# Transposing pooled k and scaled v by DMA on the sync queue instead of on TensorE

## The chip, the cores and the metric

One core of one Trainium2 chip. The metric is the device time of one execution in microseconds; lower is better. Each comparison uses runs interleaved with runs of the kernel before on the same chip.

## The reference, cut to what matters

```python
def _attn_ref(q, k, v, phi):                 # 8 batches, 8 heads, 576 rows, 64 columns, 32 memory slots
    a = softmax(phi)                         # over the 32 slots
    k_m = np.einsum('bhsm,bhsd->bhmd', a, k) # pooled k: 32 rows a head
    v_m = np.einsum('bhsm,bhsd->bhmd', a, v)
    attn = softmax(scale * np.matmul(q, k_m.transpose(0, 1, 3, 2)))
    return np.matmul(attn, v_m)

def _moe_ref(x, g_ln, w_ch1, w_ch2):         # x: the heads side by side, 512 columns
    xn = (x - mu) / np.sqrt(var + 1e-06) * g_ln
    return x + np.maximum(xn @ w_ch1, 0.0) @ w_ch2
```

The scores need k_m with its columns on the partitions, and the first layer, which the kernel merges with v_m, needs v_m the same way, scaled by the gain g_ln. So each batch needs three 128x128 transposes: two for k, one for v.

## The kernel before

The kernel works on one batch after the other and weaves the attention of batch nb into the second layer's matmuls of batch b = nb - 1. Every engine runs its instructions in the order in which they are written here, and so does the sync queue with its DMAs.

```python
def a_tr(b, ...):                      # the transposes on TensorE
    t_ps = big([P, 3, P], BF16, "kvT_ps")
    for g in range(2):
        nc.tensor.transpose(t_ps[:, g, :], s["k2"][:, g]..., ident)
    nc.tensor.transpose(t_ps[:, 2, :], s["v2"]..., ident)
    nc.vector.tensor_copy(out=kvT[:, 0:2, :], in_=t_ps[:, 0:2, :])
    nc.vector.tensor_tensor(out=kvT[:, 2, :]..., in0=t_ps[:, 2, :]..., in1=g_bf..., op=ALU.mult)
    ...
# one turn of the main loop (cut)
half(0)                                # eight matmuls of the second layer
a_kv(nb)                               # pooled k and v into PSUM, copied out
x_tiles(pr, t[0:2], False); x_tiles(pr, t[2:4], False)
phis[nb + 1] = load_phi(nb + 1)        # sync queue
load(nb + 1)                           # GpSimd queue: k, v, q of the batch after next
half(1)
a_tr(nb)
x_stats(...)
a_qT(nb + 1, 0)                        # q's transpose, a DMA on the sync queue already
half(2)
a_sc(nb)                               # scores: the first reader of kvT
...
mm2_out(pr, t[0])                      # result tile, stored from the sync queue
...
a_vb(nb)                               # products on GpSimd
```

The softmax here doesn't subtract the row's maximum and nothing guards it: scores larger than these inputs give would overflow.

Of the kernel before, what the change touches and what calls it, by code (L numbers as in the profile page):

```python
# [9 lines left out]
FP32 = mybir.dt.float32  # L10
BF16 = mybir.dt.bfloat16
AF = mybir.ActivationFunctionType
ALU = mybir.AluOpType
# [3 lines left out]
def kernel(  # L17
# [11 lines left out]
    nc = tc.nc  # L29

    B, H, S, D = q.shape
    M = phi.shape[3]
    C = H * D
    F = moe_w_ch1.shape[1]
    P = 128
# [14 lines left out]
    consts = ctx.enter_context(tc.tile_pool(name="consts", bufs=1))  # L50
    inp = ctx.enter_context(tc.tile_pool(name="inp", bufs=2))
    att = ctx.enter_context(tc.tile_pool(name="att", bufs=2))
# [3 lines left out]
    def big(shape, dtype, name):  # L56
        return psum.tile(shape, dtype, name=name, tag="big", bufs=3)

    def one(shape, dtype, name):
        return psum.tile(shape, dtype, name=name, tag="one", bufs=2)  # L60
# [8 lines left out]
    def load_phi(b, queue=None):  # L69
        t = inp.tile([P, 4, NS * M], FP32, name="phi_st")  # L70
        (queue or nc.sync).dma_start(out=t, in_=phi[b].rearrange("(j e) (p c) m -> (e p) j (c m)", e=2, p=TS))
        return t
# [23 lines left out]
    def load(b):  # L96
        loaded[b] = (phis[b] if b > 2 else load_phi(b, nc.gpsimd), load_kv(b), load_q(b))
# [16 lines left out]
    ident = consts.tile([P, P], BF16, name="ident")  # L114
# [28 lines left out]
    loaded[1] = (phi1, kv1, q1)  # L143

    g_bf = consts.tile([P, 4], BF16, name="g_bf")
    gneg = consts.tile([P, 4, P], BF16, name="gneg")
    m_sb = consts.tile([P, F], FP32, name="m_sb")

    def gain():
        g4b = consts.tile([4, P], BF16, name="g4b")  # L150
        nc.vector.tensor_copy(out=g4b, in_=g4)
        g_ps = one([P, 4], BF16, "g_ps")
        nc.tensor.transpose(g_ps, g4b, ident[0:4, 0:4])
        nc.vector.tensor_copy(out=g_bf, in_=g_ps)
        nc.vector.tensor_scalar(out=gneg, in0=g_bf.unsqueeze(2).to_broadcast([P, 4, P]),
                                scalar1=-1.0 / C, scalar2=None, op0=ALU.mult)

# [19 lines left out]
    st8 = {}  # L177
# [21 lines left out]
    def kv_mm(b, ps, sl, js=range(4)):  # L199
        e, kv = st8[b]["e"], st8[b]["kv"]  # L200
        for c in range(NS):
            for j in js:
                for g in range(2):
                    r = TS * g
                    nc.tensor.matmul(  # L205
                        ps[32 * j:32 * (j + 1), g, 0:D * (sl.stop - sl.start)],
                        e[r:r + TS, c, j, :], kv[r:r + TS, j, sl, D * c:D * (c + 1)],
                        start=(c == 0), stop=(c == NS - 1), tile_position=(r, 32 * j))

    def kv_sum(b, ps):  # L210
        e = st8[b]["e"]
        for c in range(NS):
            nc.tensor.matmul(ps[:, 0, P:P + 2], e[:, c].rearrange("p j m -> p (j m)"), ones8,
                             start=(c == 0), stop=(c == NS - 1))

    def k_out(b, k_ps, on_act):
        k2 = att.tile([P, 2, 2, D], BF16, name="k2")
        k_in = k_ps[:, :, 0:D].unsqueeze(2).to_broadcast([P, 2, 2, D])
        if on_act:
            nc.scalar.activation(out=k2, in_=k_in, func=AF.Copy)  # L220
        else:
            nc.vector.tensor_copy(out=k2, in_=k_in)  # L222
        st8[b]["k2"] = k2

    def v_out(b, v_ps):
        v2 = att.tile([P, 2, D], BF16, name="v2")
        nc.vector.tensor_copy(out=v2, in_=v_ps)
        st8[b]["v2"] = v2

    def rs_out(b, ps):  # L230
        rs = att.tile([P, 2], FP32, name="rs", bufs=4)
        nc.vector.reciprocal(out=rs, in_=ps[:, 0, P:P + 2])  # L232
        st8[b]["rs"] = rs

    def a_kv(b):
        ps = big([P, 2, 512], FP32, "kv_ps")
        if b < 2:
            kv_sum(b, ps)
        else:

            for i in range(2):
                nc.tensor.matmul(ps[:, 0, P:P + 2], st8[b]["es"][:, i, :], ones8,
                                 start=(i == 0), stop=(i == 1))
        kv_mm(b, ps, slice(0, 2))
        k_out(b, ps, b < 2)
        v_out(b, ps[:, :, D:2 * D])
        rs_out(b, ps)

    def a_tr(b, k_part=True, v_part=True):
        s = st8[b]  # L250
        t_ps = big([P, 3, P], BF16, "kvT_ps")
        if k_part:
            kvT = att.tile([P, 3, P], BF16, name="kvT")
            s["kvT"] = kvT
            for g in range(2):
                nc.tensor.transpose(t_ps[:, g, :], s["k2"][:, g].rearrange("p a d -> p (a d)"), ident)
        kvT = s["kvT"]
        if v_part:
            nc.tensor.transpose(t_ps[:, 2, :], s["v2"].rearrange("p a d -> p (a d)"), ident)  # L259
        if k_part:  # L260
            nc.vector.tensor_copy(out=kvT[:, 0:2, :], in_=t_ps[:, 0:2, :])  # L261
        if v_part:
            nc.vector.tensor_tensor(out=kvT[:, 2, :].rearrange("p (j m) -> p j m", m=M),
                                    in0=t_ps[:, 2, :].rearrange("p (j m) -> p j m", m=M),
                                    in1=g_bf.unsqueeze(2).to_broadcast([P, 4, M]), op=ALU.mult)
            rsum = att.tile([P, 2], FP32, name="rsum")
            nc.vector.tensor_reduce(out=rsum, in_=s["v2"], axis=mybir.AxisListType.X, op=ALU.add)
            s["rsum"] = rsum
# [166 lines left out]
    def mm2(pr, t, j0, j1, ps=None, finish=True):  # L435
        rT = pair[pr]
        if j0 == 0:
            chs[(pr, t)] = one([P, C], FP32, "ch_ps") if ps is None else ps
        ch_ps = chs[(pr, t)]
        for j in range(j0, j1):  # L440
            nc.tensor.matmul(ch_ps, rT[:, j, P * t:P * (t + 1)], w2b[:, j, :],  # L441
                             start=(j == 0), stop=(j == JC - 1))
        if j1 == JC and finish:
            mm2_out(pr, t)
# [113 lines left out]
    for b in range(1, B):  # L558
        pr, nb = b // 2, b + 1
        odd = b % 2  # L560
        t = [4, 5, 6, 7, 8] if odd else [0, 1, 2, 3]
        more = nb < B
        last = not more


        mm1(b, 0, 4)
        for f in late[0:1]:
            f()
        mm1(b, 4, 7)
        for f in late[1:2]:  # L570
            f()
        mm1(b, 7, JC)
        for f in late[2:]:
            f()
        late = []

        def half(i):
            if not (last and i >= 8):
                mm2(pr, t[i // 2], 8 * (i % 2), 8 * (i % 2 + 1), finish=False)

        half(0)
        if more:
            a_kv(nb)
        x_tiles(pr, t[0:2], False)
        x_tiles(pr, t[2:4], False)
        if nb + 1 < B:
            phis[nb + 1] = load_phi(nb + 1)
            load(nb + 1)
        half(1)
        if more:  # L590
            a_tr(nb)
        x_stats(pr, t[0])
        x_stats(pr, t[1])
        if nb + 1 < B:
            a_qT(nb + 1, 0)
        half(2)
        if more:
            a_sc(nb)
        x_rstd(pr, t[0:2])
        if more:  # L600
            a_w1b(nb, 0)
        mm2_out(pr, t[0])
        half(3)
        if more:
            a_den(nb, finish=False)
        mm2_out(pr, t[1])
        x_stats(pr, t[2])
        if odd or last:
            x_stats(pr, t[3])
            x_rstd(pr, t[2:4])  # L610
        half(4)
        if more:
            a_den2(nb)
        if odd:
            x_tiles(pr, t[4:5], False)
        else:
            a_w1b(nb, 1)
            a_w1b(nb, 2)
            a_w1b(nb, 3)
        if more:  # L620
            a_vb(nb)
        half(5)
        if odd or last:
            mm2_out(pr, t[2])
        if nb + 1 < B:
            a_exp(nb + 1)
        half(6)
        if odd:
            if more:
                a_w1b(nb, 1)  # L630
                a_w1b(nb, 2)
                a_w1b(nb, 3)
            x_stats(pr, t[4])
            x_rstd(pr, t[4:5])
        half(7)
        if odd:
            mm2_out(pr, t[3])
            half(8)
            half(9)
            if last:  # L640
                mm2_last(pr, t[4])
            else:
                late = [lambda pr=pr, tt=t[4]: mm2_out(pr, tt)]
        else:
            x_stats(pr, t[3])

            def tail(pr=pr, tt=t[2:4]):
                x_rstd(pr, tt)
                mm2_out(pr, tt[0])
            late = [tail, lambda pr=pr, tt=t[3]: mm2_out(pr, tt)]  # L650
# [30 lines left out]
```

## Time and profile before

| | before |
|---|---|
| time, median of 3 runs | 253.57 us (253.17 to 253.96) |
| span of the profiled run | 251.5 us |
| busy: TensorE, VectorE, ScalarE, GpSimd | 94%, 62%, 50%, 24% |
| granted TensorE clock | 1.00 |
| transposes of k and v | 24 on TensorE, 219 ns a record |
| transposes of q by DMA | 6 of 20 tiles each, 4.9 us to landing |

Landing is the time from a DMA's issue until its reader sees that it is complete. The granted clock is the share of its full clock that TensorE is given.

TensorE is busy nearly all the time, but a pipelined matmul's record is longer than the time it adds: those of the second layer last 379 ns on average and follow each other by 214 ns in the chain. What an instruction is worth is read from the chain of waits in order of time, which the prediction shows together with the DMA share around it.

### The profile page before, as it was taken

To read this page: it belongs to the slowest core of one execution; us is meant where nothing else is said; L and a number is where in the kernel's file an instruction comes from. 1 tells how busy PE (TensorE), PEld (TensorE's weight loads), DVE (VectorE), ACT (ScalarE), POOL (GpSimd) and SP (SyncE) were. 2 spreads that over 40 slices of the span, in tenths; PEclk is the share of its full clock that TensorE was granted. 3 is DMA by queue.
4 is the path that set the end of the run, shared out by engine and by line. 5 is a ranking of instruction groups with operands and counts; after the bars stand their busy time and mean duration, and the time that the engine had idled before them with its cause. 6 is when DMAs were issued, how large, how long until landed. Compare 5 with 4: busy or idle time off the path is not lost.

```text
span 251.5 us, 5775 instructions
## 1 busy us (share of the span) xinstructions
PE 236.7 (94%) x2422; PEld 133.1 (53%) x2453; DVE 154.9 (62%) x300; ACT 125.3 (50%) x213; POOL 60.0 (24%) x99
## 2 busy tenths in 40 slices
PE   7868999799999999999999999999999999999993
PEld 2533555347544665467544674467444764476453
DVE  3236772595397655967479636965679537963641
ACT  3155662587354464737363646555561755265220
POOL 8632230027204502170206302360205011000000
PEclk9999999999999999999999999999999999999999
DMA  7999999998997898639963997359871300303133
GB/s 151 194 206 206 206 256 218 281 207 122 219 191 145 155 253 189 142 43 197 241 135 80 142 252 174 85 75 231 202 145 42 80 8 0 86 16 69 44 84 83
DMA packets 41922, 36.82 MB, mean 146 GB/s; under 512 B 17444, under 2 KB 37160, under 8 KB 41896
## 3 DMA queue, kind: packets, MB, share of 16 engines
q0 software_dynamic: 17248, 19.53, 45.7%
q1 hardware_dynamic: 24488, 16.79, 28.4%
q8 instruction: 19, 0.31, 0.5%
q10 hardware_dynamic: 160, 0.13, 0.2%
q14 instruction: 7, 0.06, 0.1%
HBM read 41.42 MB, written 9.44 MB: 202 GB/s over the span
## 4 chain that ended last, share of the span: by engine, by line
PE 72%; DMA 17%; ACT 5%; DVE 2%; issue 2%; POOL 1%; POOLq 0%
PE ch_ps L441 41%; PE h_ps L372 22%; DMA q_bf<-in_q_dram 7%; DMA w2b<-in_moe_w_ch_dram 6%; ACT E_sb L313 4%; DMA kv_bf<-in_k_dram 3%; PE w1b_ps L351 2%; PE o_ps L402 2%; DVE x_sb L465 2%; PE kv_ps L205 2%; PE last_ps L453 1%; PE sc_ps L308 1%; POOL q_bf L92 1%; ACT rstd L428 1%; ACT rstd L427 0%
## 5 line engine op out<-in xcount | busy, mean ns | idle before, releaser
L441 PE MATMUL ch_ps<-w2b,rT 128*128 128x512 bf16 x531 | 123.4, 379 | 3.2 <-issue 1.7
L441 PEld LDWEIGHTS <-rT 128*128 128x128 bf16 x560 | 52.1, 98 | 63.8 <-issue 7.0
L378 ACT ACTIVATE rT<-h_ps 128x576 bf16<-128x576 f32 x88 | 52.5, 648 | 30.6 <-PE h_ps L372 30.4
L372 PE MATMUL h_ps<-Eh,w1b 128*128 128x288 bf16 x512 | 66.7, 285 | 0.7 <-ACT rT L378 0.5
L372 PEld LDWEIGHTS <-w1b 128*128 128x128 bf16 x512 | 49.6, 97 | 17.3 <-issue 1.9
L380 DVE TENSOR_SCALAR rT<-h_ps 128x576 bf16<-128x576 f32 x40 | 30.3, 758 | 30.1 <-PE h_ps L372 29.4
L355 DVE SCALAR_TENSOR_TENSOR w1b<-m_sb,rsum,w1b_ps 128x512 bf16<-128x512 f32 x64 | 43.8, 743 | 6.8 <-PE w1b_ps L351 3.8
L465 DVE SCALAR_TENSOR_TENSOR x_sb<-ch_ps,rstd,x_sb 128x512 f32<-128x512 f32 x35 | 25.6, 744 | 8.6 <-PE ch_ps L441 6.9
L408 ACT ACTIVATE x_sb<-o_ps 128x1024 f32<-128x1024 f32 (+1 forms) x20 | 17.8, 933 | 18.4 <-PE o_ps L402 18.4
L421 DVE BATCH_NORM_STATS2 bst<-x_sb 128x6 f32<-128x512 f32 x36 | 24.3, 676 | 3.1 <-ACT x_sb L408 3.1
L189 POOL TENSOR_TENSOR es<-e_sb 128x512 f32<-128x512 bf16 x6 | 6.9, 1154 | 66.2 <-ACT e_sb L182 66.2
L276 POOL TENSOR_TENSOR vb<-v,vmask 128x256 bf16<-128x256 bf16 x12 | 7.7, 662 | 59.4 <-DVE rs L232 59.4
L313 ACT ACTIVATE E_sb<-sc_ps,rs 128x640 bf16<-128x640 f32 x16 | 11.8, 790 | 19.6 <-PE sc_ps L308 19.6
L427 ACT ACTIVATE rstd<-mv,eps_sb 128x2 f32<-128x2 f32 (+1 forms) x20 | 5.9, 296 | 30.0 <-DVE mv L422 30.0
L337 DVE SCALAR_TENSOR_TENSOR Eh<-E_sb,rs,rden 128x576 bf16<-128x576 bf16 x16 | 12.4, 815 | 4.9 <-ACT rden L336 4.8
L327 ACT ACTIVATE rden<-den_ps 128x576 f32<-128x576 f32 x16 | 9.6, 648 | 3.6 <-PE den_ps L325 3.6
L174 PE MATMUL w_ps<-fill 128*128 128x512 f32 x14 | 9.2, 778 | 1.6 <-DVE fill L119 1.6
L351 PE MATMUL w1b_ps<-w1r,kvT 64*32 64x512 bf16 x256 | 10.7, 381 | 0.0
L222 DVE CAST k<-kv_ps 128x256 bf16<-128x256 f32 x7 | 3.0, 424 | 12.5 <-PE kv_ps L205 12.5
L182 ACT ACTIVATE e_sb<-phi_st 128x1152 bf16<-128x1152 f32 x8 | 9.3, 1156 | 2.6 <-DMA phi_st<-in_phi_dram 2.6
L261 DVE COPY kvT<-kvT_ps 128x256 bf16<-128x256 bf16 x8 | 2.3, 292 | 12.5 <-PE kvT_ps L259 11.8
L336 ACT ACTIVATE rden<-rden 128x576 f32<-128x576 f32 x16 | 10.0, 676 | 0.0
(69 smaller groups left out, 151.2 us busy)
## 6 DMA issues: line engine op xcount, KB each, us to landing
out_dram<-x_sb SPq DMA_DIRECT2D x70, 128.0 KB, 2.5
kv_bf<-in_k_dram POOLq DMA_DIRECT2D x7, 576.0 KB, 6.8
kv_bf<-in_v_dram POOLq DMA_DIRECT2D x7, 576.0 KB, 9.7
phi_st<-in_phi_dram SPq DMA_DIRECT2D x6, 576.0 KB, 8.9
q_bf<-in_q_dram POOLq DMA_DIRECT2D x6, 576.0 KB, 13.2
w1r<-in_moe_w_ch_dram POOLq DMA_DIRECT2D x4, 512.0 KB, 14.1
w2b<-in_moe_w_ch_dram POOLq DMA_DIRECT2D x4, 512.0 KB, 19.0
q_bf<-in_q_dram POOLq DMA_DIRECT2D x4, 288.0 KB, 12.5
```

The costliest lines, as they stand in the source:

```text
L313: nc.scalar.activation(out=E_[:, g].rearrange("p (a x) -> p a x", a=2), in_=sc[:, :, 0:HP], func=AF.Exp, scale=s["rs"][:, g:g + 1])
L336: nc.scalar.activation(out=rd[:, g], in_=rd[:, g], func=AF.Exp, scale=-1.0)
L337: nc.vector.scalar_tensor_tensor(out=Eh[:, g, :], in0=s["E"][:, g, 0:S], scalar=s["rs"][:, g:g + 1], in1=rd[:, g].rearrange("p a x -> p (a ...
L351: nc.tensor.matmul(ps[32 * j:32 * (j + 1), g, :], s["kvT"][r:r + 64, 2, 32 * j:32 * (j + 1)], w1r[r:r + 64, j, fs], start=True, stop=True, ...
L355: nc.vector.scalar_tensor_tensor(out=s["w1b"][:, g, fs], in0=m_sb[:, fs], scalar=s["rsum"][:, g:g + 1], in1=ps[:, g, :], op0=ALU.mult, op1 ...
L372: nc.tensor.matmul(h_ps[:, half, 0:HS], s["w1b"][:, g, P * j:P * (j + 1)], s["Eh"][:, g, HS * half:HS * (half + 1)], start=(g == 0), stop= ...
L378: nc.scalar.activation(out=dst, in_=h_ps[:, :, 0:HS], func=AF.Relu)
L380: nc.vector.tensor_scalar(out=dst, in0=h_ps[:, :, 0:HS], scalar1=0.0, scalar2=None, op0=ALU.max)
L408: nc.scalar.activation(out=x[:, 0:n].rearrange("p i (u y) -> p i u y", u=2), in_=o_ps.rearrange("p u (i y) -> p i u y", i=2)[:, 0:n], func ...
L421: nc.vector.bn_stats(out=stt, in_=x)
L441: nc.tensor.matmul(ch_ps, rT[:, j, P * t:P * (t + 1)], w2b[:, j, :], start=(j == 0), stop=(j == JC - 1))
L465: nc.vector.scalar_tensor_tensor(out=x, in0=ch_ps, scalar=rstd, in1=x, op0=ALU.mult, op1=ALU.add)
```

## The change

The intent is to take eighteen transposes off the engine that bounds the kernel and give them to the DMA engines, for batches 2 to 7. Since the gain g_ln multiplied the transposed v, a broadcast gB of it is built once, so that v is scaled before the transpose. Cut to its core:

```diff
+        sel = consts.tile([4, 4, M], BF16, name="sel")
+        ...
+        nc.vector.tensor_copy(out=gB, in_=gb_ps)
@@ a_kv
-        k_out(b, ps, b < 2)
+        if b < 2:
+            k_out(b, ps, True)
+            ...
+            return
+        kvg = att.tile([P, 3, P], BF16, name="kvg")
+        nc.vector.tensor_copy(out=kvg[:, 0:2]..., in_=ps[:, :, 0:D]...)
+        nc.vector.tensor_tensor(out=kvg[:, 2]..., in0=ps[:, :, D:2 * D], in1=gB..., op=ALU.mult)
         v_out(b, ps[:, :, D:2 * D])
         rs_out(b, ps)
+        s["kvT"] = att.tile([P, 3, P], BF16, name="kvT")
+        nc.sync.dma_start_transpose(out=s["kvT"], in_=kvg.rearrange("p n x -> p (n x)"))
+        ...
@@ main loop
         half(1)
-        if more:
-            a_tr(nb)
```

More of the change, by code (lines that the diff above doesn't have):

```diff
@@ L145 @@
     g_bf = consts.tile([P, 4], BF16, name="g_bf")
+    gB = consts.tile([P, P], BF16, name="gB")
     gneg = consts.tile([P, 4, P], BF16, name="gneg")
@@ L154, in gain @@
         nc.vector.tensor_copy(out=g_bf, in_=g_ps)
+        sel = consts.tile([4, 4, M], BF16, name="sel")
+        nc.vector.tensor_copy(out=sel, in_=ident[0:4, 0:4].unsqueeze(2).to_broadcast([4, 4, M]))
+        gb_ps = one([P, P], FP32, "gb_ps")
+        nc.tensor.matmul(gb_ps, sel.rearrange("p j m -> p (j m)"), g4b, start=True, stop=True)
+        nc.vector.tensor_copy(out=gB, in_=gb_ps)
         nc.vector.tensor_scalar(out=gneg, in0=g_bf.unsqueeze(2).to_broadcast([P, 4, P]),
@@ L244, in a_kv @@
         kv_mm(b, ps, slice(0, 2))
-        k_out(b, ps, b < 2)
+        if b < 2:
+            k_out(b, ps, True)
+            v_out(b, ps[:, :, D:2 * D])
+            rs_out(b, ps)
+            return
+        kvg = att.tile([P, 3, P], BF16, name="kvg")
+        nc.vector.tensor_copy(out=kvg[:, 0:2].rearrange("p g (a d) -> p g a d", a=2),
+                              in_=ps[:, :, 0:D].unsqueeze(2).to_broadcast([P, 2, 2, D]))
+        nc.vector.tensor_tensor(out=kvg[:, 2].rearrange("p (g d) -> p g d", g=2),
+                                in0=ps[:, :, D:2 * D], in1=gB.rearrange("p (g d) -> p g d", g=2),
+                                op=ALU.mult)
         v_out(b, ps[:, :, D:2 * D])
         rs_out(b, ps)
+        s = st8[b]
+        s["kvT"] = att.tile([P, 3, P], BF16, name="kvT")
+        nc.sync.dma_start_transpose(out=s["kvT"], in_=kvg.rearrange("p n x -> p (n x)"))
+        s["rsum"] = att.tile([P, 2], FP32, name="rsum")
+        nc.vector.tensor_reduce(out=s["rsum"], in_=s["v2"], axis=mybir.AxisListType.X, op=ALU.add)
     def a_tr(b, k_part=True, v_part=True):
```

## The prediction

> **What bounds the kernel now.** I read, in this order, the page's chain, the chain in order of time, the timeline of one batch, the DMA share by microsecond, and landing times by window. First the chain by engine:
>
> ```profile
> PE 72%; DMA 17%; ACT 5%; DVE 2%; issue 2%; POOL 1%; POOLq 0%
> ```
>
> The DMA part is the loading phase up to 46.7 us; after it TensorE sets the end, and a removed instruction pays only what it holds of this chain. One batch (the one whose k and v sums start at 94.4 us) in order of time; columns are start, length, what:
>
> ```profile
> 94.50 0.73 PE kv_ps L205 x72
> ...
> 95.95 1.67 PE ch_ps L441 x7
> 97.62 0.11 PE kvT_ps L256 x2
> 97.73 0.06 PE kvT_ps L259
> 97.79 1.73 PE ch_ps L441 x8
> 99.52 0.31 PE sc_ps L308 x8
> ...
> 99.85 1.48 ACT E_sb L313 x2
> 101.33 0.19 ACT rstd L427
> ```
>
> The three transposes hold 0.11 + 0.06 = 0.17 us. Between them and the scores (sc_ps) lie eight matmuls of the second linear layer. The scores are the first reader of kvT, and all that follows (exponential, rstd, the release of the accumulator) hangs on them. So a late kvT delays everything by as much as it is late. The timeline shows when data for a transposing DMA exist, and a transposing DMA that the kernel already has:
>
> ```profile
> 95.29 0.42 DVE L222 CAST k<-kv_ps 128x256 bf16<-128x256 f32 x1 [1.75 <-PE kv_ps L205]
> 95.63 0.28 DVE L227 CAST v<-kv_ps 128x128 bf16<-128x128 f32 x1
> 97.83 0.29 DVE L261 COPY kvT<-kvT_ps 128x256 bf16<-128x256 bf16 x1 [1.84 <-PE kvT_ps L259]
> 97.97 3.19 SPq L287 DMA_TRANSPOSE qT<-q_bf  x1
> 98.03 0.28 DVE L263 TENSOR_TENSOR kvT<-kvT_ps,g_bf 128x128 bf16<-128x128 bf16 x1
> 99.44 0.14 PEld L308 LDWEIGHTS <-kvT 64*32 64x32 bf16 x16 [0.42 <-DVE bst L421]
> ```
>
> The scores load weights at 99.44; k is out of PSUM by 95.71. The DMA engines around it (last two columns: busy share, GB/s):
>
> ```profile
> 97.00:98.00 1.00, 1.00 (x8) 0.56 (x7) 0.17 (x1) 0.55 (x1) 0.35 (x1) 1.00 0.68 214
> 98.00:99.00 1.00, 1.00 (x7) 0.47 (x5) 1.00 (x4) 0.00 (x0) 0.00 (x0) 1.00 0.00 0
> 99.00:100.00 1.00, 1.00 (x27) 0.27 (x25) 0.93 (x4) 0.15 (x1) 0.00 (x0) 1.00 0.86 167
> ```
>
> With nothing else in flight the q transpose issued at 97.97 moves nothing for a microsecond. And what a backlog of loads does to 128 KB stores (median issue to landing, last column), first one window with a backlog, then one without:
>
> ```profile
> out_dram<-x_sb SPq DMA_DIRECT2D x4, 128.0 KB, 6.8
> out_dram<-x_sb SPq DMA_DIRECT2D x8, 128.0 KB, 2.4
> ```
>
> So a small transfer on the sync queue takes 2.4 us on idle engines and 6.8 behind the GpSimd queue's loads.
>
> **What the Trainium skill says.** "VectorE: DVE Perf Modes", section "The three transpose paths", gives 390 ns for a TensorE transpose of 128x128 bf16 and 1309 ns by DMA. Here a TensorE one has 219 ns in its record and costs 0.06 us of the chain, being pipelined; the 20-tile q transpose is issued in 3.19 us and lands after 4.9, or 160 ns a tile plus 1.7 us: both figures depend on company. "DMA: Bandwidth & Descriptors", section "Latency and other measured facts", has a first byte after about 600 ns for the hardware queues; this trace shows about 1.1 us (issue 97.97, first packets about 99.05), and I use that. The same page, "Queues, rings and completion order", says that each DMA engine goes round-robin over the queues that have work, packet by packet. The packet records agree once a queue is being served (27 packets of one and 28 of the other in a quarter microsecond), but not at entry: stores issued at 114.02 show their first packet at 117.75, 3.7 us later, while the loads' queue took every slot. The change puts both kinds of transpose on one queue, so no serialization of two transposing streams comes in.
>
> **The change part by part.** It concerns six batches (numbers 2 to 7); 0 and 1 keep TensorE.
> - Removed from TensorE: 3 transposes and 3 weight loads a batch, 0.17 us of the chain each time, 6 x 0.17 = 1.0 us. That is all the direct gain there is.
> - Removed from VectorE: the kvT copy (292 ns) and the gain multiply (281 ns). Added: one multiply from PSUM of the same 128x128 size, estimated 0.28 us. Net about 0.3 us less a batch, off the chain (VectorE is 62% busy). The statistics can start earlier, but rstd on ScalarE queues behind E_sb, so no gain.
> - PSUM: one allocation of the three-buffer ring less. The scores then reuse the buffer of the k and v sums, free by about 96.2: no new wait.
> - Start: a small matmul and two VectorE copies, a few tenths at 7 us, before a 0.53 us wait for q; the chain there is DMA. Nothing.
> - Added: one DMA of 3 tiles a batch. Data ready: 95.29 + 0.34 (start of the second operation) + 0.28 = 95.91, issue about 96.0. Quiet engines: 1.1 to the first packet, 3 x 0.16 = 0.5 of transfer, about 0.6 to the semaphore (the q transpose's last packet at 102.2, landing at 102.87): 2.2 us, landing at 98.2. TensorE arrives at 99.44 - 0.17 = 99.3. Slack 1.1 us: hidden, if quiet.
> - Moved: on the sync queue, which is in order, the load of the next phi now comes behind kvT. It went out at 61.9, 89.4, 116.6, 144.8 and 172.0 before; now about 5 to 7 us later in each batch's course. The exponential that reads it starts at 77.4, 104.5, 132.8, 159.9 and 188.1, so with the shortest landing of a phi load, 3.9 us, the tightest (issued about 96.7, read at 104.5) has some 4 us left. And the GpSimd queue's loads, which shared the engines with phi, end sooner.
>
> That last point decides whether the engines are quiet. Before, the loads of k, v and q end at about 97.3, 123.0, 151.2 and 178.3 in batches 3 to 6. From the packets left when phi began, at the unshared rate of 90 per half microsecond, they would end near 96.0, 122.4, 150.3 and 177.4. First packets of kvT would come at about 97.1, 123.0, 152.4 and 178.2 (data ready plus 0.1 plus 1.1). All four just behind the end of the backlog, so quiet; batch 7 has no loads beside it (share 0.00). I take no stall for these five.
>
> Batch 2 differs: data ready at 66.3, while loads fill the engines until 74.5 (share 1.24 at 66 to 67), about 72.5 without phi. There I take the stores' 3.7 us to a first packet, so about 70.1, then 24 packets on each engine, between 0.5 us (served together) and 3.0 (each alternating with a 107 ns load packet), then 0.6: landing 71.2 to 73.7, middle 72.3. TensorE wants it at 69.93 - 0.17 = 69.8. Stall about 2.5 us (1.4 to 3.9).
>
> Sum: -1.0 + 2.5 = +1.5 us. Four slacks of about a microsecond that rest on drain times known to half a microsecond will sometimes fail, so I set the centre at 255.0 us, against 253.57 before.
>
> **The rivals.**
> - All hidden, batch 2 too: for it speaks that the q transpose of 58.4 us did get most packets through before the loads took over, and that packet-wise alternation should let a small transfer pass; against it, that transpose's landing of 8.9 us in place of 4.9, and every store under a backlog needing 5.7 us or more. It would give 253.57 - 1.0 = 252.6.
> - Contention in every loaded batch: if loads already handed to the engines still fill them when kvT arrives in batches 3 to 6, each lands 1 to 4 us later, stalls of 0 to 3 us. With 1.2 us each in four batches: 255.0 + 4.8 = 259.8, slower by over 2%. For it: the margins are 0.6 to 2.1 us and estimated. Against: phi leaves the competition, and the loads move with the chain.
> - Transposes cost TensorE more than the chain says (weight loads 98 ns, records of 219 ns, restart of the stream). At the full 3 x 0.219 us a batch it would be 3.9 us: 249.6 without stalls, still within 2%. Against: sixteen 512-column matmuls and the transposes together take 3.57 us of chain (95.95 to 99.52), and the matmuls alone 16 x 0.214 = 3.42 (0.214 from the chain's stretch at 79.66, 5.13 us for three halves of eight); 0.15 is left.
> - A delayed phi holding up ScalarE: needs a landing after 8 us in batch 3, beside engines that I expect idle; it would add 1 to 2 us. Unlikely.
>
> **Range and chances.** Low end: all hidden, 252.5. High end: batch 2 at its worst (3.9) and about 0.4 us in each of five others, 253.6 - 1.0 + 3.9 + 2.0 = 258.5. Faster by over 2% (below 248.5) needs five times the gain that the chain offers: 0.02. Slower by over 2% (above 258.6) is the second rival: 0.13. Within 2%: 0.85.
>
> **What would show it.** The chain should lack the kvT_ps lines, and in batches 3 to 7 go from sixteen ch_ps matmuls straight to sc_ps, with kvT landing 2.1 to 2.5 us after issue. In batch 2 a DMA wait of 1.4 to 3.9 us should stand before sc_ps, with a landing of 5 to 7 us. The phi loads should be issued 5 to 7 us later relative to the chain, with no ScalarE wait for phi. I am wrong if sc_ps waits for kvT in most batches (the engines were not quiet, or the fixed part of a transpose is larger than 1.7 us), or if batch 2 shows no wait (small transfers do pass a backlog), or if the time falls below 252.

## The result, and the profile after

| | before | after |
|---|---|---|
| time, median of 4 fast runs | 253.39 us | 258.01 us (257.87 to 258.06) |
| ratio | | 1.0178 (1.0159 to 1.0197) |
| span of the profiled run | 251.5 us | 256.1 us |
| granted TensorE clock, mean of the profiled run | 1.00 | 0.993 |

Ratios here and below are the mean time of one kernel's fast runs over that of the other's of the same rounds, so not quite the ratio of the medians. Executions over 1.5% slower than the fastest of the same kernel are left out of the means. The changed kernel is 4.6 us slower.

The same stretch of the chain as in the prediction, of the changed kernel (columns: start, length, what). It is the batch numbered 3:

```profile
99.82 0.76 PE kv_ps L212 x72
...
101.03 0.21 DVE kvg L260
101.24 0.03 issue
101.26 3.40 PE ch_ps L463 x15
104.66 0.35 PE sc_ps L330 x8
...
105.03 1.48 ACT E_sb L335 x2
```

The sixteen matmuls (one record is missing) run straight into the scores. The stretch from their start to the scores takes 104.66 - 101.26 = 3.40 us, against 99.52 - 95.95 = 3.57 before: the 0.17 us of the transposes are gone. Where the scores of each batch begin in the two chains (batch 2: their weight loads):

| batch | before | after | shift |
|---|---|---|---|
| 2 | 69.93 | 73.86 | +3.93 |
| 3 | 99.52 | 104.66 | +5.14 |
| 4 | 125.38 | 130.40 | +5.02 |
| 5 | 154.90 | 159.74 | +4.84 |
| 6 | 180.77 | 185.44 | +4.67 |
| 7 | 210.28 | 214.78 | +4.50 |

From batch 3 on each batch wins 0.12 to 0.18 us. All of the loss comes in batch 2 and in the few microseconds after it. The timeline there, after the change (start, length, engine, line, what, and in brackets the idle time just before and what ended it):

```profile
66.26 1.18 SPq L267 DMA_TRANSPOSE kvT<-kvg  x1
...
66.37 3.40 PE L463 MATMUL ch_ps<-w2b,rT 128*128 128x512 bf16 x15 [0.16 <-issue]
...
73.86 0.14 PEld L330 LDWEIGHTS <-kvT 64*32 64x32 bf16 x16 [4.59 <-DMA kvT<-kvg]
73.86 0.47 PE L330 MATMUL sc_ps<-qT,kvT 64*32 64x320 bf16 x16 [4.10 <-DMA kvT<-kvg]
...
74.48 3.17 PE L463 MATMUL ch_ps<-w2b,rT 128*128 128x512 bf16 x8
...
78.16 1.62 PEld L463 LDWEIGHTS <-rT 128*128 128x128 bf16 x8
```

And the same batch in the kernel before:

```profile
69.93 0.14 PEld L308 LDWEIGHTS <-kvT 64*32 64x32 bf16 x16 [0.42 <-DVE bst L421]
...
70.55 1.69 PE L441 MATMUL ch_ps<-w2b,rT 128*128 128x512 bf16 x7
...
73.07 1.89 PE L441 MATMUL ch_ps<-w2b,rT 128*128 128x512 bf16 x8
```

kvT is issued at 66.26 and lands after 7.6 us; TensorE stands still for 4.10 us. Then eight matmuls that took 1.69 us before (one record is missing there) take 3.17. The windows of the changed kernel say why (after the window and its length: busy time and instructions of TensorE, its weight loads, VectorE, ScalarE, GpSimd; the last three columns are granted clock, DMA share, GB/s; the share adds up the times of packets, and goes over 1 where they overlap):

```profile
68.00:70.00 2.00, 1.77 (x9) 0.59 (x6) 0.75 (x2) 0.00 (x0) 0.00 (x0) 1.00 1.22 211
70.00:72.00 2.00, 0.00 (x0) 0.00 (x0) 0.00 (x0) 0.00 (x0) 0.00 (x0) 1.00 1.21 197
72.00:74.00 2.00, 0.14 (x8) 0.14 (x16) 0.00 (x0) 0.00 (x0) 0.00 (x0) 1.00 1.16 254
74.00:76.00 2.00, 2.00 (x29) 0.74 (x16) 1.38 (x2) 1.70 (x4) 0.00 (x0) 0.74 0.51 172
76.00:78.00 2.00, 2.00 (x7) 0.84 (x6) 1.09 (x3) 0.16 (x1) 0.00 (x0) 0.50 0.45 87
78.00:80.00 2.00, 1.95 (x10) 0.91 (x9) 1.93 (x5) 1.19 (x2) 0.00 (x0) 0.91 1.17 217
```

The DMA engines are full until 74, and after the idle stretch the granted clock falls to half for 3.4 us (the three windows lack 0.26, 0.50 and 0.09 of two microseconds each, 1.7 us in all; the clock's own record has 0.50 from 74.95 to 78.36). From the scores' weight loads to the second layer's third accumulator it takes 78.16 - 73.86 = 4.30 us, against 73.07 - 69.93 = 3.14 before: 1.2 us. Between the scores of batches 2 and 3 the shift grows by 1.21 us although that stretch also wins 0.17, so 1.4 us in all.

Counting the packet records of that stretch by kind and half microsecond shows how kvT gets in (1152-byte packets are the loads', 256-byte ones transposes', 4-byte ones completions; zero places left out):

```
 from   loads 1152 B   kvT 256 B   completions of the sync queue
 68.5       87             -            -
 69.0       87             -            -
 69.5       85             -            -
 70.0       67            47            -
 70.5       72            66            -
 71.0       66            67            -
 71.5       74            72            -
 72.0       69            69            -
 72.5       75            58           16
 73.0       43             5           16
```

The first packet comes 3.8 us after the issue (at 70.04), and then the transpose advances by as many 256-byte packets as the loads by their own: 384 packets, 24 on each of 16 engines, take 3.2 us (to 73.26).

The sum, -1.0 (six times 0.17) + 4.1 + 1.4 = +4.5 us, is the measured 4.6. The chain of the changed kernel's page also gives 5% to stores; at those points TensorE was busy and the shift table shows no loss, so I read nothing into it.

### The profile page after: what moved, and what is told of

The parts are those of the page before. It is cut to its first block, busy times and chain, and to the rows that moved or that the text cites. A ratio compares the mean times of both kernels' runs of the same rounds, so it can differ in the third digit from the quotient of the medians.

```text
span 256.1 us, 5753 instructions
## 1 busy us (share of the span) xinstructions
PE 237.8 (93%) x2405; PEld 132.8 (52%) x2436; DVE 154.1 (60%) x296; ACT 125.3 (49%) x213; POOL 60.1 (23%) x99
## 4 chain that ended last, share of the span: by engine, by line
PE 64%; DMA 24%; ACT 4%; DVE 4%; issue 1%; POOL 1%; SPq 0%; POOLq 0%
PE ch_ps L463 38%; PE h_ps L394 18%; DMA q_bf<-in_q_dram 7%; DMA w2b<-in_moe_w_ch_dram 6%; DMA out_dram<-x_sb 5%; DMA kv_bf<-in_k_dram 3%; DMA kvT<-kvg 3%; ACT E_sb L335 3%; PE w1b_ps L373 2%; DVE x_sb L487 2%; PE last_ps L475 1%; PE kv_ps L212 1%; PE sc_ps L330 1%; DVE kvg L258 1%; PE den_ps L347 1%
## 5 line engine op out<-in xcount | busy, mean ns | idle before, releaser
L463 PE MATMUL ch_ps<-w2b,rT 128*128 128x512 bf16 x531 | 124.7, 382 | 3.4 <-issue 0.9
L463 PEld LDWEIGHTS <-rT 128*128 128x128 bf16 x560 | 52.8, 98 | 65.6 <-issue 7.8
L181 PE MATMUL w_ps<-fill 128*128 128x512 f32 x14 | 9.8, 818 | 1.6 <-DVE fill L119 1.6
L258 DVE CAST kvg<-kv_ps 128x256 bf16<-128x256 f32 x6 | 2.5, 424 | 10.5 <-PE kv_ps L212 10.5
L92 POOL DMA_DIRECT2D q_bf<-in_q_dram x10 | 7.6, 758 | 4.2 <-DMA w2b<-in_moe_w_ch_dram 1.8
## 6 DMA issues: line engine op xcount, KB each, us to landing
w2b<-in_moe_w_ch_dram POOLq DMA_DIRECT2D x4, 512.0 KB, 19.4
```

Source lines behind the costliest of these rows:

```text
L463: nc.tensor.matmul(ch_ps, rT[:, j, P * t:P * (t + 1)], w2b[:, j, :], start=(j == 0), stop=(j == JC - 1))
```

## The experiments

The theory: batch 2's kvT is late because GpSimd's loads for batch 3 fill the engines, and the idle TensorE then gets a lower clock. Rivals: a transposing DMA costs something in every batch; the first one is slow by itself; the lower clock comes from the DMA. The changed kernel itself was run again on two other chips: ratios 1.0235 and 1.0201.

**e1_batch2_on_pe and e1_again: batch 2 back on TensorE.**

```diff
-        if b < 2:
-            k_out(b, ps, True)
+        if b < 3:
+            k_out(b, ps, b < 2)
@@ main loop
         half(1)
+        if nb == 2:
+            a_tr(nb)
```

> Batch 2 back on TensorE, batches 3 to 7 by DMA. Theory (the whole loss is batch 2's late landing plus the clock that drops after it; each other batch gains 0.17 us): 253.4 - 5 x 0.17 = 252.6 us, no wait for kvT over 0.1 us, granted clock 1.0. Rival (a transposing DMA costs something in every batch, a sixth of the 4.6 us each): 253.4 + 5 x 0.77 = 257.2 us.

> Batch 2 on TensorE, 3 to 7 by DMA, again on another chip: ratio to before 0.997 (252.5 us), no wait over 0.2 us. If the gain was chance: 1.000.

Measured: 252.30 us against 253.22, ratio 0.9970 (0.9953 to 0.9987), and on another chip 252.35 against 253.25, ratio 0.9972 (0.9956 to 0.9988). In the first profile no wait for kvT stood in front of the scores' matmuls; in the second one of 0.5 us did, in batch 3 (landing 3.9 us), so the margin there is thin, and the expected "no wait over 0.2 us" did not hold. The five other batches gain what the prediction said; the rival of a cost in each batch falls. This version beats the kernel before by 0.3%, and with it the changed one.

**e2_only_batch2_dma: the reverse.** The conditions above become `b != 2` and `more and nb != 2`.

> Only batch 2 by DMA, the others on TensorE. Theory: 253.4 - 0.17 + 4.1 of wait + 1.4 of lower clock = 258.7 us, the wait for kvT about 4 us, granted clock down to 0.5 for a few us after it. Rival (loss spread over the batches): 253.4 + 0.8 = 254.2 us.

Measured: 259.44 us (258.82 to 259.76), ratio 1.0247; landing 7.6 us, wait 4.1, clock 0.50 from 74 to 78 us. One transposing DMA out of six does all the damage. It is 0.7 us above the expectation: the lower clock lasted longer (0.56 from 72 to 74, 0.73 from 78 to 80). By the clock's record it was 6.8 us here and in r_after, and 3.4 us in the profiles of the changed kernel, e3, e5, e6 and e9; what decides between the two is not settled.

**e3_loads_after_vb: the loads of batch 3 issued after kvT of batch 2.** GpSimd's products of batch 2 need its v and so hold GpSimd's queue back:

```diff
+        if nb == 2:
+            a_vb(nb)
         if nb + 1 < B:
             phis[nb + 1] = load_phi(nb + 1)
             load(nb + 1)
@@
-        if more:
+        if more and nb != 2:
             a_vb(nb)
```

> All six batches by DMA as in the changed kernel, but GpSimd's loads of k, v and q for batch 3 are issued after its vb products of batch 2, so some 9 us later and behind kvT's transpose. Theory (the backlog of those loads makes batch 2 late): kvT of batch 2 lands after 2.2 to 3.3 us in place of 7.6, no clock drop, time 253.4 - 1.0 = 252.4 us. Rival (the first such transpose, or the q transpose ahead of it in the same queue, is slow by itself): still about 258.0 us.

Measured: batch 2's landing falls from 7.6 to 3.2 us and TensorE no longer waits there. The backlog is shown as its cause; the first such transpose is not slow by itself. But the time is 257.95 us (256.23 to 258.71), not 252.4. The wait moved to batch 3. The timeline of this run:

```profile
69.83 0.47 PE L330 MATMUL sc_ps<-qT,kvT 64*32 64x320 bf16 x16
...
81.20 3.80 SPq L309 DMA_TRANSPOSE qT<-q_bf  x1
...
85.09 7.34 SPq L492 DMA_DIRECT2D out_dram<-x_sb  x9
...
102.11 0.47 PE L330 MATMUL sc_ps<-qT,kvT 64*32 64x320 bf16 x16 [2.87 <-DMA kvT<-kvg]
```

q of batch 3 now arrives late, its transpose waits on the in-order sync queue until 81.20 (76.00 after the change), and nine stores pile up behind it, to be moved at 90 to 98 us, beside the loads for batch 4. kvT of batch 3 then found a backlog: landing 6.2 us, wait 2.9, and the clock down again (0.50 from 104 to 106).

**e7_loads_and_qT_late: the same, with the q transpose behind the first four stores.**

```diff
-        if nb + 1 < B:
+        if nb + 1 < B and nb != 2:
             a_qT(nb + 1, 0)
@@
         half(5)
+        if nb == 2:
+            a_qT(nb + 1, 0)
```

> As e3_loads_after_vb (loads of batch 3 behind batch 2's kvT), and in that batch the next q transpose comes after the first four stores on the sync queue, in place of ahead of them, so that stores do not pile up behind its wait for q. Theory (in e3 the wait moved to batch 3 because delayed stores filled the loads' window): landings of 2.2 to 3.5 us in all six batches, no wait over 0.3 us, clock 1.0, time 253.4 - 1.0 = 252.4 us. Rival (later loads alone make batch 3 late): a wait of 2 to 3 us in batch 3 again, 256 to 258 us.

Measured: 255.73 us, but the six runs lie apart, from 253.48 to 256.92; ratio 1.0093 (1.0049 to 1.0137). The profiled run, the fastest, lands batch 3 after 4.1 us with a wait of 1.4. Against the kernel before, e3 lost 4.7 us and e7 loses 2.8, so two fifths come back, not all. In the profile kvT of batch 3 stands behind six stores (issued from 92.24 to 95.98), whose packets run until 98, so the traffic that was put off still meets it; what the slower runs waited for has no record. (The profile's mean clock of 0.993 comes from a drop at 16.0 to 19.4 us, in the loading phase, and not from batch 3.) Neither the theory's 252.4 nor the rival's 2 to 3 us of wait holds for it.

**e5_k_only: two tiles instead of three in batch 2.** v's tile goes by TensorE.

```diff
-        nc.sync.dma_start_transpose(out=s["kvT"], in_=kvg.rearrange("p n x -> p (n x)"))
+        ...
+        n = 2 if b == 2 else 3
+        nc.sync.dma_start_transpose(out=s["kvT"][:, 0:n], in_=kvg[:, 0:n].rearrange("p n x -> p (n x)"))
+        ...
@@ main loop
         half(1)
+        if nb == 2:
+            a_tr(nb, k_part=False)
```

> In batch 2 only the two k tiles go by DMA, v's tile by TensorE; batches 3 to 7 as in the changed kernel. Theory (2.7 us until the loads let it in, then about one 256-byte packet per load packet, 3.1 us for 24 packets per engine): a third of the alternating part goes, landing 6.6 us in place of 7.6, wait for kvT 3.1 us, time 258.0 - 1.0 = 257.0, or 255.8 if the shorter wait also spares the clock. Rival (a fixed delay, whatever the size): landing 7.6, time 258.0 us.

Measured: landing 6.6 us, wait 2.88, 256.54 us (254.81 to 257.45). The landing shrinks by 0.9 us, about a third of 3.2, as it should if the transpose alternates with the loads; the first packet is at 70.1, as before. The fixed delay falls as the only cause. The clock still dropped in the profiled run (0.50 from 74 to 76); the fastest run, 254.81 us, kept a mean clock of 0.998.

**e6_phi_ahead: phi ahead of kvT on the sync queue**, on top of e1.

```diff
         half(0)
+        if nb + 1 < B:
+            phis[nb + 1] = load_phi(nb + 1)
         if more:
             a_kv(nb)
@@
         if nb + 1 < B:
-            phis[nb + 1] = load_phi(nb + 1)
             load(nb + 1)
```

> Batch 2 on TensorE (252.3 us when last run) and the next phi loaded ahead of kvT's transpose on the sync queue, as before the change. The prediction held that kvT is quiet because phi went behind it. From where phi's packets ended before the change (97.6, 124.1, 152.2, 179.4) kvT would land 1.2 us later, near 98.8, 125.3, 153.4 and 180.6, against a need at about 99.3, 125.2, 154.7 and 180.6: waits of 0 to 0.3 us in batches 4 and 6, landings of 3 to 4 us, time 252.3 to 252.9. If phi's place is what decides: waits of 1 us and more in three or four batches, 255 us or over.

Measured: 257.69 us (257.22 to 259.00, the slow run left out) against 252.95, ratio 1.0175. The profile is of the slowest of the fast runs, 259.00; the other five had a mean clock of 0.997 or more, so theirs is a loss by waits and not by the clock. The waits of the profiled run (who waited for whom; us in total, times, longest):

```profile
PE sc_ps L330 <- DMA kvT<-kvg: 5.3, 3, 2.4
```

Landings of 5.7, 4.7, 2.8, 5.1 and 2.6 us in batches 3 to 7, and waits in batches 3, 4 and 6. My expectation was too low, and the prediction's point, that phi's new place behind kvT keeps those batches quiet, holds more strongly than I had worked out. In batch 3 the packet records show the last 24 of the 384 packets about a microsecond after the rest, with the DMA share down at 0.29. 24 packets are one engine's share, and the records show what most likely held it: an 8 KB packet of an instruction queue runs from 98.25 to 100.23, and kvT's last completions come at 100.22 and 100.23. No run takes such a packet away.

**e4_fill and e4_fill_2: the wait filled with matmuls that nobody reads**, on top of the changed kernel.

```diff
         half(2)
+        if nb == 2:
+            f_ps = big([P, 2, 512], FP32, "f_ps")
+            for _ in range(17):
+                nc.tensor.matmul(f_ps[:, 0, :], w2b[:, 0, 0:P], w2b[:, 1, :], start=True, stop=True)
         if more:
             a_sc(nb)
```

> The changed kernel with 17 matmuls of 512 columns that nobody reads put ahead of batch 2's scores (17 x 0.214 = 3.6 us of the 4.1 us wait). kvT still lands late, so the wait itself stays lost. Theory (TensorE's idle time makes the granted clock drop, worth about 1.4 us): clock 1.0 throughout, 258.0 - 1.4 = 256.6 us. Rival (the lower clock comes from something else or costs nothing): 258.0 us with the clock still down.

> The changed kernel once more, as the yardstick of this chip: ratio to before 1.018 to 1.024, wait of 4 to 5 us in batch 2, lower clock after it.

> The filling matmuls again, beside the changed kernel on the same chip, because the first time they were compared across chips and the gain was smaller than expected (257.2 against 258.0 us). Theory (idle time lowers the clock): no lowered clock after batch 2, and 1.0 to 2.0 us less than the changed kernel in the same rounds. Rival (filling saves nothing): the same as the changed kernel within 0.3 us.

Measured: 257.23 us (ratio 1.0165), and beside the changed kernel 257.60 (1.0176) against 258.11 (1.0201). The windows of the first run show no drop:

```profile
70.00:72.00 2.00, 2.00 (x11) 0.92 (x10) 0.00 (x0) 0.00 (x0) 0.00 (x0) 1.00 1.21 194
72.00:74.00 2.00, 1.52 (x15) 0.55 (x21) 0.00 (x0) 0.00 (x0) 0.00 (x0) 1.00 1.18 256
74.00:76.00 2.00, 1.84 (x30) 0.85 (x27) 1.35 (x2) 1.67 (x4) 0.00 (x0) 1.00 0.53 175
```

From the scores' weight loads to the third accumulator it is now 77.03 - 73.90 = 3.13 us, so the 1.2 us of that stretch are back. From the scores of batch 2 to those of batch 3 it takes 103.31 - 73.90 = 29.41 us, against 104.66 - 73.86 = 30.80 in the changed kernel: that is the 1.4 us of the lower clock. But only 0.5 to 0.8 us arrive at the end, and beside the changed kernel on the same chip the intervals overlap: kvT of batch 6 now lands after 4.2 and 4.4 us and TensorE waits 0.7 and 1.0 us there.

The r_after run, made beside e5 to e7, was the other repeat of the changed kernel:

> The changed kernel again, for the same chip and rounds: 258.0 us, ratio 1.018, one wait for kvT of about 4 us in batch 2.

Measured: 258.96 us, ratio 1.0235. Its kvT of batch 2 landed after 8.4 us, TensorE waited 4.9, and the clock was at 0.59 to 0.50 from 72 to 78 us. From these scores to those of batch 3 it took 31.45 us, 2.0 more than the 29.42 of the kernel before less its transposes, so here the lower clock cost 2.0 us.

**e8_pool_wait and e9_pool_wait_long: idle time without a transposing DMA of k and v.** The kernel before, with a needless chain of copies on GpSimd in batch 2 ahead of the scores:

```diff
@@ a_tr
+        if b == 2:
+            late = att.tile([P, 3, P], BF16, name="kvT_late", bufs=1)
+            for _ in range(9):                       # 4 in e8
+                nc.gpsimd.tensor_copy(out=late, in_=kvT)
+            s["kvT"] = late
```

> The kernel before, all transposes on TensorE, but in batch 2 GpSimd copies kvT four times over (a needless chain of some 4 us) before the scores may read it: an idle TensorE without any DMA transpose. Theory (idle alone lowers the clock): wait of w = 3 to 4.5 us, granted clock near 0.5 for 3 to 5 us after it, time 253.2 + w + 1 to 2 us. Rival (the clock fell because of the DMA): time 253.2 + w, clock 1.0.

> As e8_pool_wait with nine copies in place of four: five more of 0.55 us, so a wait of 1.1 + 2.8 = 3.9 us for TensorE in batch 2, without any DMA transpose of k and v. Theory (TensorE's idle time alone lowers the clock, once it is long enough; 1.1 us was not): granted clock near 0.5 for 3 to 7 us after the wait, time 253.2 + 3.9 + 1.2 to 2.3 = 258.3 to 259.4 us. Rival (the transposing DMA or the DMA load lowers it): clock 1.0, time 257.1 us.

Measured: e8's copies were shorter than I thought, and TensorE waited 1.13 us. The time was 254.39 us against 253.25, so +1.1 us, with the clock at 1.00: a short wait costs itself and no more. e9 waited 3.97 us and took 258.61 us (258.50 to 259.61) against 253.35: +5.3 us, of which 4.0 are the wait. Its windows:

```profile
70.00:72.00 2.00, 0.00 (x0) 0.00 (x0) 0.48 (x2) 0.00 (x0) 1.82 (x4) 1.00 1.16 229
72.00:74.00 2.00, 0.12 (x8) 0.12 (x16) 0.00 (x0) 0.00 (x0) 1.82 (x5) 1.00 1.22 210
74.00:76.00 2.00, 2.00 (x30) 0.84 (x23) 1.36 (x2) 1.68 (x4) 1.08 (x2) 0.83 0.36 61
76.00:78.00 2.00, 2.00 (x8) 0.91 (x7) 1.42 (x3) 0.32 (x2) 0.00 (x0) 0.50 0.32 62
78.00:80.00 2.00, 2.00 (x10) 0.80 (x8) 1.68 (x5) 1.27 (x3) 0.00 (x0) 0.82 1.17 216
```

The same fall to half the clock, with no kvT DMA in the program. Together with e4, where the same late DMA with a busy TensorE left the clock alone, this shows that TensorE's idle time lowers it, and that 4 us of idle cost 1.3 us more than themselves (by the profile 1.4: from the scores of batch 2 to those of batch 3 it takes 30.98 us, against 29.59 before).

## Why the prediction was wrong, and where it was right

It gave 255.0 us where 258.0 were measured: a loss of 1.5 us in place of 4.6. The place and the cause of the loss were right: batch 2, whose transpose comes behind the loads. Two terms of the sum failed, one too small by 1.6 us and one missing, 1.4 us; 1.5 + 1.6 + 1.4 is 4.5. The centre of 255.0 was the bare sum, 253.57 + 1.5: nothing was added for the slacks that "will sometimes fail". That 258.0 lies inside the range, up to 258.5, and within 2% is partly luck: the range got there with 0.4 us of waits in each of five batches, which the changed kernel doesn't show, and not with a lower clock.

- **The gain, 6 x 0.17 = 1.0 us: right.** The shift table shows 0.12 to 0.18 us a batch, and e1 gains 0.9 us with five batches (0.85 worked out).
- **Hidden in batches 3 to 7: right in the changed kernel, with thinner margins than drawn.** Landings there were 2.3 to 3.3 us in place of 2.2 (2.1 to 2.5 in the signs); only batch 5 came to 2.3. The first packet comes 1.2 us after the issue, not 1.1: that of the q transpose issued at 97.97 is at 99.17, which was read as 99.05. Part of the rest goes with something that the prediction didn't count, packets of the instruction queue (below). No wait of those batches exceeds 0.1 us on TensorE in the changed kernel's first profile, but e1_again shows one of 0.5, and e4 waits of up to 1.0.
- **Phi's new place: right that it matters, as e6 shows** by taking it away (+5.4 us over e1's median).
- **Batch 2's wait, 2.5 us: too small.** This is the first term that failed. The entry delay of 3.7 us, taken from the stores, was right (3.8). The transfer was given "between 0.5 us (served together) and 3.0 (each alternating)" and put in the middle; the packet records show the alternating case, 3.2 us, and e5 confirms it by removing a third. So a landing of 7.6 us, where 5 to 7 was given, and a wait of 4.1, just past the range's end of 3.9.
- **The lower clock: missing.** The sum had the wait as its only cost. The Trainium skill, in "TensorE: Matmul & The Clock Gate", section "Why this matters for your kernels", warns of TensorE idle gaps of more than about 3 us between bursts of matmuls. I did not connect it with a predicted wait of 1.4 to 3.9 us. Here waits of 2.4 (e6), 2.9 (e3, e5), 4.0 (e9), 4.1 and 4.9 us were followed by a clock near 0.5 in the profiles, so gaps below the page's 3 us did it too, and waits of 1.1 to 1.6 us (e8, e7, e6's others) were not. It need not be so in every execution: five runs of e6 and one of e5, whose waits are not on record, kept a mean clock of 0.997 or more. In the changed kernel it came to 1.4 us in the first profile and 2.0 in r_after.
- **The start, the PSUM buffer, ScalarE's wait for phi: as predicted**, nothing; the chain has no such piece, and ScalarE's one wait for phi is the first load's, as before. The phi loads went out 5.6 to 8.5 us later relative to the chain, where 5 to 7 was said.

The rival "contention in every loaded batch" is not what the changed kernel shows, though e3, e6 and e7 show how near it is: each shifts some traffic and brings it about. Why single landings vary is in part on record. In the profiles used here batches 5 and 7 have no loads and stores beside kvT. In batch 5, where no 16 KB packet of the instruction queue was under way later than 0.5 us after the issue, nine profiles give 2.3 us eight times and 2.4 once. In batch 7 such a packet (0.9 to 1.4 us long) always is, and the landing follows its end in ten profiles: 2.4 us where it ends 0.90 us after the issue, 2.5 at 1.01, 2.7 at 1.15, 2.9 at 1.34 to 1.41. So one instruction packet appears to hold up a whole transpose; no experiment removed it, so this is not shown as the cause. The hole of a microsecond in the loads and kvT of r_after (72 to 73 us), whose kvT landed after 8.4, stays open.

## What to carry to other kernels

Before giving an on-chip operation to a DMA, ask what else fills the DMA engines at the moment of its issue: here three tiles landed after 2.3 us on idle engines and after 7.6 to 8.4 us behind bulk loads, while the removed operations had held only 0.17 us of the chain. Count a wait that TensorE spends idle for some microseconds as the wait plus the matmuls that then run at a lower clock. And when moving loads to make room, follow the in-order queue to the next stage: e3 removed the wait from one batch and put it into the next.

## What the Trainium skill lacked or had wrong

- "DMA: Bandwidth & Descriptors", section "Latency and other measured facts": a first byte of about 600 ns for hardware queues; the transposing DMAs here, on idle engines, show first packets about 1.2 us after issue (batch 5: issue 156.40, first packet 157.61, landing 2.3 us after issue).
- The same page, section "Queues, rings and completion order": round-robin by packets fits the equal counts of the records once a queue is served, but the page lacks the delay until it is: 3.7 us from issue to first packet behind GpSimd's loads in a store at 114.02 us of the kernel before, and 3.8 in kvT at 66.26 of the changed one. And a transpose in 256-byte packets gained one packet per 1152-byte load packet, so 98 KB took 3.2 us.
- "VectorE: DVE Perf Modes", section "The three transpose paths": compares single durations (390 ns on TensorE, 1309 ns by DMA). What decided here is absent: 0.06 us of chain for a pipelined TensorE transpose, and 2.3 to 8.4 us to landing for a DMA of three tiles, by the traffic beside it.
- No page has what an instruction queue's 16 KB packet does to a DMA beside it: landings of a three-tile transpose on otherwise idle engines went from 2.4 to 2.9 us with the end of that packet, 0.90 to 1.41 us after the issue.
